# Attention inside a bias stage: two steps there instead of three, loads issued later, the first ten steps in another order

## The chip, the core and the metric

The program runs on one core of a Trainium2 chip. The core has engines that each take their own instructions strictly in the order in which the program lists them: TensorE (PE, its weight loads shown as PEld), VectorE (DVE), ScalarE (ACT), GpSimd (POOL), and the sync engine (SP), which here issues nearly all DMAs. [...] The metric is the device time of one execution in microseconds (us); lower is better.

## What is computed

An attention with a learned position bias, and a two-layer block behind it. Cut to what matters:

```python
B, H, S, D = 4, 8, 576, 64
scores = matmul(q, k.T) / sqrt(D)
psi_rel = log1p(abs(i - j));  psi_i = log1p(max(i, 1))
h = maximum((psi_rel / psi_i)[..., None] @ w1 + b1, 0)      # 32 hidden values for each (i, j)
scores = scores + (h @ w2)                                  # one bias for each head and (i, j)
attn = exp(scores - max); attn = attn / (sum(attn) + 1e-9)
x = (attn @ v), heads side by side                          # 2304 tokens x 512
out = (mish-like gate of (x @ w_in)) @ w_out
```

The bias depends on the head, not on the batch, so it is made once and used four times.

## The kernel before

**Bias stage.** The 576 rows are taken in 36 tiles of 16 rows (`idx` 0 to 35 in the loop at L545 to L567, in the order of `ts`). For tile `idx` four hidden tiles `ht` are made (`make_h`, L524 on VectorE or L522 on ScalarE; a small planner with prices, L508 to L516, decides which: 123 fall to VectorE and 21 to ScalarE), TensorE multiplies them with `w2t` into a PSUM tile `bps` (L554), and `evac` takes that out in two pieces, a left one (L535 on ScalarE; for the last two tiles L533 on VectorE) and a right one (L536, ScalarE), into `bt`, which SP writes to DRAM (`bias_d`, L541). There are two `bps` buffers and eight `bt` buffers. `make_h` runs two tiles ahead of TensorE, `evac` one tile behind it. The bias comes back in five loads, one for each chunk c of 128 query rows (chunk 4 has 64 rows), in the order c = 0, 1, 4, 2, 3 (`load_bias`, three DMAs each). Such a load reads what other DMAs wrote, so SP waits until those writes have landed before it issues it, and everything behind it in SP's list waits too.

**Attention.** The 16 pairs of heads (i; four batches times four head pairs) times five chunks c give 80 steps n. A step has these parts, and the text below calls them so: *scores* (L226 on TensorE, into two PSUM tiles `s`, of which there is just one pair), *reductions* (`add_bias`, L243 on VectorE: adds the bias, takes the row extremes, frees the `s` tiles), *exps* (L258 on ScalarE, two for c < 4, one for c = 4), *turn* (`transposes`, L296 on TensorE, two steps later, then two copies from PSUM, L305, or four smaller ones for c = 4), *ends* (L321, the last 64 columns, and a copy L322), and *products* (`pv_duo`, L335 and L339, on TensorE, into a single PSUM tile `o`, copied out by L342). The c = 0 and 1 of a pair form group 0, the others group 1; each group's products need all of its turns. Turned tiles `main` and `tail` have one buffer for each group, turned PSUM tiles `tp` three, and the tile `pt` of a step with c < 4 three. The three first pairs multiply in plain fp32.

**What sets the order.** The order is written out by hand: the loop of the bias stage places steps 0 to 2 at the tiles in `SOFT_AT` (scores at that tile, reductions one tile later, exps two tiles later), loads at the tiles in `BIAS_AT` and at `load_raw(0)`, `load_raw(1)` (q, k and v of a pair); after it, `step(n)` issues the parts of each step. `split` puts one piece of the conversion of the MLP weights (L125 to L132 on VectorE, L142, L143) into each step from step 5 on, and `ahead` the loads for later pairs.

Of the kernel before, what the change touches and what calls it, by code (L numbers as in the profile page):

```python
# [45 lines left out]
def kernel(ctx: ExitStack, tc, qk, v, wb, w2, w_in, w_out, psia, psi4, rinv, eye, out):  # L46
# [46 lines left out]
    todo, w64, w32 = list(order), [], []  # L93
# [115 lines left out]

    NPAIR = B * HP  # L210
    steps = [(i, c) for i in range(NPAIR) for c in ORDER]
    NS = len(steps)
    pt_t, live, o_t, sums = {}, {}, {}, {}

# [3 lines left out]
    def scores(n):  # L218
        i, c = steps[n]
        hi, lo = qk_t[i]  # L220
        terms = [(hi, hi)] if i < PLAIN else [(hi, hi), (hi, lo), (lo, hi)]
        live[n] = [s_ps.tile([P, 2, 512], F32, name="s") for _ in range(2)]
        for j in range(2):
            for t, (q, k) in enumerate(terms):
                for s, rows in zip(live[n], (TOP, LOW)):
                    pe.matmul(s[:, j, :SH], q[rows, c * P:(c + 1) * P], k[rows, KO + j * SH:KO + (j + 1) * SH],  # L226
                              start=(t == 0), stop=(t == len(terms) - 1))

    def add_bias(n):

        i, c = steps[n]
        bt = bias_t[i // B, c]
        m = st.tile([P, 2], F32, name="m")
        if c < 4:
            pt = pp.tile([P, 2 * S], F32, name="pt")
        else:
            pt = p4p.tile([P, 640], F32, name="pt4")
        for u, s in enumerate(live[n]):
            if c < 4:
                rows, k, sl = slice(0, P), u, slice(u * S, (u + 1) * S)  # L240
            else:
                rows, k, sl = (TOP, LOW)[u], 0, slice(0, S)
            dve.tensor_tensor_reduce(  # L243
                out=halves(pt[rows, sl]), in0=s[rows, :, :SH], in1=halves(bt[rows, sl]),
                scale=-0.125, scalar=BIG, op0=ALU.add, op1=ALU.min, accum_out=m[rows, k:k + 1])
        live[n] = (pt, m)
# [13 lines left out]
    def reciprocals(i):  # L260

        hp, b = divmod(i, B)
        r = sums.pop(i)
        rr = r_pad[i % 2]
        dve.tensor_scalar(r, r, 1e-9, None, op0=ALU.add)
        dve.reciprocal(rr[:, 0:9], r)
        rt = xs.tile([P, 32], F32, name="rt", bufs=2)
        dve.transpose(rt, rr)
        for g in range(4):
            sp.dma_start(out=r_d[b][hp][:, 32 * g:32 * g + 32], in_=rt[32 * g:32 * g + 9])  # L270
# [9 lines left out]
    def place(c):  # L280
        return (0, c * P) if c < 2 else (1, 64 + (c - 2) * P)

    def transposes(n, shared=False):
        i, c = steps[n]
        pt, m = live[n]
        main, tail = turned(i, 0 if c < 2 else 1)
        top, low = (t_ps.tile([P, 512], F32, name="tp") for _ in range(2))
        if c < 4:
            cols = [h * 640 + k * P for h in range(2) for k in range(4)]
        else:  # L290
            cols = [k * P for k in range(4)] + [S - P]
        for k, c0 in enumerate(cols):
            for rows, tp in ((TOP, top), (LOW, low)):
                if c == 4 and rows == LOW:
                    c0 = 64 + k * P if k < 4 else 0
                pe.transpose(tp[:, k * 64:k * 64 + 64], pt[rows, c0:c0 + P], ident[rows, rows])  # L296
        inline = c in (2, 3) or (c < 2 and i == 0)
        if inline:
            copy_end = ends(n)
        if c < 4:  # L300
            off = place(c)[1]
            for g, tp in enumerate((top, low)):
                q0 = off + 64 * g
                copy = dve.tensor_copy if shared and g else act.copy
                copy(main[:, :, :, q0:q0 + 64], tp.rearrange("p (h k q) -> p h k q", h=2, k=4))  # L305
            if inline:
                copy_end()
        else:
            for h, tp in enumerate((top, low)):
                act.copy(main[:, h, :, 0:64], tp[:, :256].rearrange("p (k q) -> p k q", k=4))  # L310
                act.copy(tail[(TOP, LOW)[h], 0:64], tp[(LOW, TOP)[h], 256:320])

    def ends(n):

        i, c = steps[n]
        pt, m = live[n]
        grp, off = place(c)
        tail = turned(i, grp)[1]
        end = t_ps.tile([P, 512], F32, name="tp")
        for h in range(2):  # L320
            pe.matmul(end[h * 64:h * 64 + 64, 0:P], pt[:, 512 + 64 * h:576 + 64 * h], ident, start=True, stop=True)  # L321
        return lambda: act.copy(tail[:, off:off + P], end[:, 0:P])  # L322
# [26 lines left out]
    LAG = 2  # L349
# [25 lines left out]
    def ahead(n):  # L375

        i, x = divmod(n, 5)
        if x == 0 and i + 1 < NPAIR:
            load_raw(i + 1)
        c = {(1, 3): 0, (2, 1): 1, (2, 3): 2, (3, 2): 4, (3, 4): 3}.get((i % B, x))  # L380
        if c is not None and i // B + 1 < HP:
            load_bias(i // B + 1, c)
        if n == NS - 11:
            load_x(0, x0.tile([P, HP, TB], F32, name="xraw"))
        if n == NS - 10:
            x_hi[0], x_lo[0] = (xa_t[:, t].bitcast(F32R) for t in range(2))
            load_r(0, x_lo[0].bitcast(F32), 0, HP)
        if NS - 5 <= n < NS - 1:
            d = n - (NS - 5)
            x, hi, lo = (y[0][:, d] for y in (x_raw, x_hi, x_lo))  # L390
            dve.tensor_tensor(hi, x, lo.bitcast(F32), op=ALU.mult)
            pool.tensor_tensor(x, x, lo.bitcast(F32), op=ALU.mult)
            pool.tensor_tensor(lo, x, hi.bitcast(F32), op=ALU.subtract)
# [9 lines left out]
    def convert(on_act, last):  # L403
# [3 lines left out]
        elif conv and next(conv[0]):  # L407
            conv.clear()
            load_weights()
            if w32 and w32[0][0] in order[:EARLY]:  # L410
                split_weights(pool)

    def step(n):
        i, x = divmod(n, 5)

        def begin():
            if n < NS:
                scores(n)
                add_bias(n)

        def turn():
            if 0 <= n - LAG < NS:
                transposes(n - LAG)
            if x == 4 and i:
                ends(n - 3)()

        def end():
            if 0 <= n - 1 < NS and (n - 1) % 5 == 4:
                reciprocals((n - 1) // 5)
            if n < NS:  # L430
                ahead(n)
                split(n)

        def products():
            todo = {4: (i, 0, (0, 1)), 0: (i - 1, 0, (2, 3) if i < NPAIR else (2, 3, 4)), 1: (i - 1, 0, (4,) if i < NPAIR else ()), 2: (i - 1, 1, (0, 1, 2)),
                    3: (i - 1, 1, (3, 4))}.get(x, (-1, 0, ()))
            j, grp, ks = todo
            if 0 <= j < NPAIR and (j, grp) != (0, 0):
                for k in ks:
                    pv_duo(j, grp, k)  # L440

        if n in (3, 4):
            scores(n)
            if n == 3:
                transposes(0, True)
            add_bias(n)
            exps(n, 0)
            if n == 3:
                transposes(1, True)
            exps(n, 1)  # L450
            if n == 3:
                transposes(2)
            else:
                for k in range(5):
                    pv_duo(0, 0, k)
            end()
            return
        begin()
        turn()
        if n < NS:  # L460
            exps(n, 0)
            exps(n, 1)
        end()
        products()
        if x == 1 and n < NS:
            ends(n - 1)()

# [30 lines left out]

    spent = {"v": 0.0, "a": 0.0}
    maker = {}  # L500
    SOFT_AT = (18, 27, 32)
    BIAS_AT = (12, 20, 24, 30, 37)
    for idx, t in enumerate(ts):
        spent["a"] += 1.0 + (1.9 if idx in SOFT_AT else 0.0)
        spent["v"] += (1.7 if idx in SOFT_AT else 0.0)
        n = reach(t)[2]
# [39 lines left out]
    for idx in range(NB + 2):  # L546
        if idx < NB:
            t = ts[idx]
            make_h(idx + 2)
            n = reach(t)[2]  # L550
            ps = bps.tile([P, 1024], F32, name="bps")
            for a in range(0, n, 512):
                for cg in range(4):
                    pe.matmul(ps[cg * 32:cg * 32 + 32, a:min(a + 512, n)], w2t,  # L554
                              h_t[idx, cg][:, a:min(a + 512, n)], start=True, stop=True)
            bps_t[t] = ps
        if 1 <= idx <= NB:
            evac(idx - 1)
        if idx == 1:
            load_raw(0)  # L560
        if idx in BIAS_AT:
            load_bias(0, ORDER[BIAS_AT.index(idx)])
        for lag, do in enumerate((scores, add_bias, exps)):
            if idx - lag in SOFT_AT:
                for u in range(2 if lag == 2 else 1):
                    do(SOFT_AT.index(idx - lag), *((u,) if lag == 2 else ()))
        if idx == 14:  # L567
            load_raw(1)
    load_weights()
    bias_scope.close()  # L570
# [316 lines left out]
```

## Time and profile before

| | us |
|---|---|
| median of 3 runs | 673.56 |
| lowest and highest of them | 670.41, 674.48 |
| the profiled execution | 672.85 |
| its span, first to last instruction | 670.9 |
| granted TensorE clock, mean over the span | 0.992 |

The profiled execution took 672.85 us, of which 670.9 are the span that the views show; 1.95 lie outside it. Times in the views count from the start of the span. The bias stage fills roughly the first 58 us, then come the other steps of the attention, and the MLP last.

### The profile page before, as it was taken

To read this page: it belongs to the slowest core of one execution; us is meant where nothing else is said; L and a number is where in the kernel's file an instruction comes from. 1 tells how busy PE (TensorE), PEld (TensorE's weight loads), DVE (VectorE), ACT (ScalarE), POOL (GpSimd) and SP (SyncE) were. 2 spreads that over 40 slices of the span, in tenths; PEclk is the share of its full clock that TensorE was granted. 3 is DMA by queue.
4 is the path that set the end of the run, shared out by engine and by line. 5 is a ranking of instruction groups with operands and counts; after the bars stand their busy time and mean duration, and the time that the engine had idled before them with its cause. 6 is when DMAs were issued, how large, how long until landed. Compare 5 with 4: busy or idle time off the path is not lost.

```text
span 670.9 us, 13799 instructions
## 1 busy us (share of the span) xinstructions
PE 646.0 (96%) x5300; PEld 498.6 (74%) x5300; DVE 449.6 (67%) x821; ACT 412.2 (61%) x871; POOL 150.2 (22%) x142
## 2 busy tenths in 40 slices
PE   6878999999999999999999999999999999999997
PEld 3214667777777777778888998788888888888886
DVE  7995777877888785631423364344599877888884
ACT  6995899989999899762433333344474444454441
POOL 0000133333222332601111121102233321133330
PEclk9979999999999999999999999999999999999999
DMA  4997586677667859107448886624664544443300
GB/s 138 303 315 234 170 251 208 212 236 237 219 213 231 271 155 265 33 19 218 150 160 241 260 229 189 210 103 135 211 190 125 157 158 142 144 128 114 101 32 32
DMA packets 100913, 119.65 MB, mean 178 GB/s; under 512 B 15600, under 2 KB 77296, under 8 KB 100848
## 3 DMA queue, kind: packets, MB, share of 16 engines
q1 hardware_dynamic: 98544, 110.59, 52.4%
q0 software_dynamic: 1872, 8.09, 4.0%
q8 instruction: 41, 0.67, 0.4%
q14 instruction: 24, 0.20, 0.1%
q10 hardware_dynamic: 432, 0.09, 0.1%
HBM read 79.47 MB, written 39.28 MB: 177 GB/s over the span
## 4 chain that ended last, share of the span: by engine, by line
PE 81%; DMA 7%; DVE 5%; ACT 4%; issue 2%; SPq 1%; POOL 0%; DVEq 0%; ACTq 0%
PE h L623 27%; PE s L226 10%; PE y L739 8%; PE o L335 8%; PE h L739 8%; PE tp L296 5%; PE y L740 4%; PE h L740 4%; PE tp L321 3%; PE bps L554 3%; DVE ht L524 2%; DMA xa<-r_d 2%; PE o L339 2%; DMA x_d<-x 1%; DMA bias_d<-bt 1%
## 5 line engine op out<-in xcount | busy, mean ns | idle before, releaser
L258 ACT ACTIVATE pt<-pt,m 128x576 f32<-128x576 f32 x144 | 112.1, 789 | 3.6 <-DVE m L243 3.6
L243 DVE CUSTOM_DVE_ANT_0 pt<-s,bias 128x576 f32<-128x576 f32 (+1 forms) x112 | 81.6, 755 | 37.2 <-PE s L226 30.9
L635 ACT ACTIVATE g<-h 128x512 f32<-128x512 f32 x72 | 42.8, 597 | 75.9 <-PE h L623 64.2
L305 ACT COPY main<-tp 128x512 f32<-128x512 f32 x126 | 68.0, 596 | 22.1 <-PE tp L296 22.0
L335 PE MATMUL o<-main,vt 128*64 128x320 f32 (+1 forms) x512 | 74.3, 412 | 0.0
L177 POOL TENSOR_TENSOR qklo<-rawqk,qkhi 128x304 fp32r<-128x304 f32 x52 | 44.0, 871 | 123.5 <-DMA rawqk<-in_qk_dram 115.6
L639 POOL TENSOR_TENSOR g<-g 128x256 f32<-128x256 f32 (+1 forms) x40 | 33.7, 844 | 159.9 <-ACT g L635 151.0
L623 PE MATMUL h<-xa,lc 128*128 128x512 f32 (+1 forms) x288 | 55.5, 354 | 0.0
L296 PEld LDWEIGHTS tp<-ident,pt 64*128 64x128 f32 x1184 | 51.3, 138 | 4.2 <-ACT main L305 1.7
L296 PE MATMUL tp<-ident,pt 64*128 64x64 f32 x1184 | 52.7, 222 | 1.4 <-ACT main L305 1.3
L722 DVE TENSOR_TENSOR gslot<-w,gslot 128x1024 fp32r<-128x1024 f32 x30 | 43.3, 1455 | 15.4 <-ACT gslot L721 15.4
L623 PEld LDWEIGHTS h<-xa,lc 128*128 128x128 f32 x288 | 47.6, 189 | 7.5
L554 PE MATMUL bps<-ht,w2t 128*32 128x512 f32 (+17 forms) x352 | 38.7, 559 | 14.5 <-ACT bt L536 6.1
L722 DVE TENSOR_TENSOR gslot<-quarters,gslot 128x1024 fp32r<-128x1024 f32 x28 | 47.0, 1705 | 7.9 <-ACT gslot L721 7.9
L721 ACT CAST gslot<-w 128x1024 fp32r<-128x1024 f32 x30 | 31.5, 1051 | 30.2 <-DVE w L718 18.2
L721 ACT CAST gslot<-quarters 128x1024 fp32r<-128x1024 f32 x28 | 29.4, 1052 | 32.5 <-DVE quarters L718 20.4
L226 PE MATMUL s<-qkhi 64*128 64x288 f32 x260 | 49.2, 343 | 0.1
L226 PEld LDWEIGHTS s<-qkhi 64*128 64x128 f32 x260 | 28.1, 184 | 25.8 <-DVE m L243 11.0
L335 PEld LDWEIGHTS o<-main,vt 128*64 128x64 f32 x512 | 32.7, 136 | 16.0 <-issue 0.7
L524 DVE TENSOR_SCALAR ht<-at,bb 128x576 f32<-128x576 f32 (+17 forms) x123 | 44.1, 440 | 0.0
L226 PE MATMUL s<-qklo,qkhi 64*128 64x288 f32 x260 | 42.0, 296 | 0.0
L226 PE MATMUL s<-qkhi,qklo 64*128 64x288 f32 x260 | 41.2, 292 | 0.4 <-POOL qklo L177 0.4
(150 smaller groups left out, 1479.4 us busy)
## 6 DMA issues: line engine op xcount, KB each, us to landing
g_d<-g SPq DMA_DIRECT2D x32, 512.0 KB
bias_d<-bt SPq DMA_DIRECT2D x36, 295.5 KB
w<-in_w_in_dram SPq DMA_DIRECT2D x16, 512.0 KB
w<-in_w_out_dram SPq DMA_DIRECT2D x16, 512.0 KB
quarters<-g_d SPq DMA_DIRECT2D x16, 512.0 KB
qkhi<-in_qk_dram POOLq DMA_DIRECT2D x13, 608.0 KB, 4.6
rawqk<-in_qk_dram SPq DMA_DIRECT2D x13, 608.0 KB
w<-g_d SPq DMA_DIRECT2D x15, 512.0 KB
```

Of the source, the lines that this page charges most:

```text
L226: pe.matmul(s[:, j, :SH], q[rows, c * P:(c + 1) * P], k[rows, KO + j * SH:KO + (j + 1) * SH], start=(t == 0), stop=(t == len(terms) - 1))
L243: dve.tensor_tensor_reduce(out=halves(pt[rows, sl]), in0=s[rows, :, :SH], in1=halves(bt[rows, sl]), scale=-0.125, scalar=BIG, op0=ALU.add, ...
L258: act.activation(ps, ps, AF.Exp, bias=m[:, u:u + 1], scale=-1.0, accum_out=sums[i][:, k:k + 1])
L296: pe.transpose(tp[:, k * 64:k * 64 + 64], pt[rows, c0:c0 + P], ident[rows, rows])
L305: copy(main[:, :, :, q0:q0 + 64], tp.rearrange("p (h k q) -> p h k q", h=2, k=4))
L335: pe.matmul(o[h * 64:h * 64 + 64, :w], vt[:, h, k, :], main[:, h, k, :], start=(k == 0), stop=False, **kw)
L524: dve.tensor_scalar(ht[:, :n], at[:, :n], bb[:, k:k + 1], 0.0, op0=ALU.add, op1=ALU.max)
L554: pe.matmul(ps[cg * 32:cg * 32 + 32, a:min(a + 512, n)], w2t, h_t[idx, cg][:, a:min(a + 512, n)], start=True, stop=True)
L623: pe.matmul(h[:, u * n:(u + 1) * n], w_at(f, d)[t], x[:, d, :n], start=(k == 0), stop=(k == 11))
L721: act.copy(hi, src)
L722: dve.tensor_tensor(lo, src, hi.bitcast(F32), op=ALU.subtract)
L739: pe.matmul(o, hi[:, f], wc[m][:, f], start=(f == 0 and m in (0, 1, 3)), stop=False, **kw)
```

## The change

Steps 0 and 1 alone stay in the bias stage, at the tiles 26 and 33 (before: steps 0, 1, 2 at 18, 27, 32). The bias loads move from the tiles 12, 20, 24, 30, 37 to 18, 25, 31, 36, 37, `load_raw(0)` from tile 1 to 12, `load_raw(1)` from 14 to 34. The first ten steps run in the order (pair, chunk) = (0,0), (0,1), (0,4), (1,0), (1,1), (0,2), (0,3), (1,4), (1,2), (1,3) instead of all of pair 0 and then all of pair 1, so chunks 2 and 3 of the bias are first needed at steps 5 and 6 (before: 3 and 4). A new function `opening` issues the steps 2 to 9. The first turns of pairs 0 and 1 have one of their two copies on VectorE, ahead of or behind the reductions. `load_raw(2)` moves from step 5 to step 6. The planner's table counts two steps instead of three and gives as many hidden tiles to each engine as before.

```diff
+    FIRST = 10
+    steps[:FIRST] = [(0, 0), (0, 1), (0, 4), (1, 0), (1, 1), (0, 2), (0, 3), (1, 4), (1, 2), (1, 3)]
...
-    def transposes(n, shared=False):
+    def transposes(n, inline=None, shared=False):
...
-        inline = c in (2, 3) or (c < 2 and i == 0)
+        if inline is None:
+            inline = c in (2, 3)
...
-        if x == 0 and i + 1 < NPAIR:
+        if (n == 6 if i < 2 else x == 0) and i + 1 < NPAIR:
...
+    def opening(n):
+        scores(n)
+        if n < 4:
+            transposes(n - 2, True, True)
+        add_bias(n)
+        if n == 4:
+            transposes(2)
+        if n == 5:
+            for k in (3, 4):
+                pv_duo(0, 0, k)
+        if 5 <= n <= 8:
+            transposes(n - 2, n >= 7, True)
+        exps(n, 0)
+        exps(n, 1)
+        if n == 7:
+            reciprocals(0)
+        ahead(n)
+        split(n)
+        if n == 6:
+            for m in (3, 4):
+                ends(m)()
+        for j, grp, k in {4: [(0, 0, k) for k in range(3)],
+                          7: [(1, 0, k) for k in range(2)],
+                          8: [(1, 0, k) for k in range(2, 5)],
+                          9: [(0, 1, k) for k in range(5)]}.get(n, ()):
+            pv_duo(j, grp, k)
...
+        if n < FIRST:
+            opening(n)
+            return
...
+        if n == FIRST:
+            transposes(7)
...
-    SOFT_AT = (18, 27, 32)
-    BIAS_AT = (12, 20, 24, 30, 37)
+    SOFT_AT = (26, 33)
+    BIAS_AT = (18, 25, 31, 36, 37)
...
-        if idx == 1:
+        if idx == 12:
             load_raw(0)
...
-        if idx == 14:
+        if idx == 34:
             load_raw(1)
```

ScalarE inside the bias stage, around the two exps of step 0 (`pt,sums<-pt,m`). Before, they stand between the evacuations (`bt<-bps`) of the tiles 19 and 20:

```order
L535 ACTIVATE bt<-bps,rinv_t 128x575
L536 ACTIVATE bt<-bps,rinv_t 128x16
L258 ACTIVATE pt,sums<-pt,m 128x576 x2
L522 ACTIVATE ht<-at,bb 128x320
L535 ACTIVATE bt<-bps,rinv_t 128x271
L536 ACTIVATE bt<-bps,rinv_t 128x320
```

After, they stand between those of the tiles 27 and 28:

```order
L540 ACTIVATE bt<-bps,rinv_t 128x383
L541 ACTIVATE bt<-bps,rinv_t 128x208
L260 ACTIVATE pt,sums<-pt,m 128x576 x2
L527 ACTIVATE ht<-at,bb 128x448
L540 ACTIVATE bt<-bps,rinv_t 128x399
L541 ACTIVATE bt<-bps,rinv_t 128x192
```

What moved is the place, eight tiles later; in both an exps pair and one hidden tile are ahead of an evacuation.

ScalarE at the end of the bias stage: the right pieces of the last two tiles (128x96 and 128x80), and the copies of step 0's turn (`main<-tp`). Before, the one exp of step 2 stands ahead of both pieces:

```order
L536 ACTIVATE bt<-bps,rinv_t 128x112
L258 ACTIVATE pt_830,sums<-pt_830,m 128x576
L536 ACTIVATE bt<-bps,rinv_t 128x96
L536 ACTIVATE bt<-bps,rinv_t 128x80
L305 COPY main_889<-tp 128x8x64
L322 COPY tail_890<-tp 128x128
```

After, the two exps of step 1 stand between the pieces:

```order
L541 ACTIVATE bt<-bps,rinv_t 128x112
L541 ACTIVATE bt<-bps,rinv_t 128x96
L260 ACTIVATE pt,sums<-pt,m 128x576 x2
L541 ACTIVATE bt<-bps,rinv_t 128x80
L308 COPY main_878<-tp 128x8x64
L325 COPY tail_879<-tp 128x128
```

What moved is that the last piece of the last tile now follows two exps, and step 2 is no more there.

TensorE in the steps 9 to 11, from one step's scores (`s<-qklo`) to the next. Before, the products (`o<-main`) of group 0 of pair 1 are dealt out over the steps:

```order
L226 MATMUL s<-qklo 128x288 x4
L296 MATMUL tp<-ident,pt_1089 128x64 x10
L321 MATMUL tp<-ident,pt 64x128 x2
L335 MATMUL o<-main_1076,vt 64x256 x4
L226 MATMUL s<-qklo 128x288 x4
L296 MATMUL tp<-ident,pt 128x64 x16
L321 MATMUL tp<-ident,pt 64x128 x2
L335 MATMUL o<-main_1076,vt 64x256 x4
L226 MATMUL s<-qklo 128x288 x4
```

After, all products of group 1 of pair 0 stand between the scores of steps 9 and 10, and two turns (of steps 7 and 8) between those of 10 and 11:

```order
L228 MATMUL s<-qklo 128x288 x4
L338 MATMUL o<-main_956,vt 64x320 x8
L342 MATMUL o<-tail_957,vt 64x320 x2
L228 MATMUL s<-qklo 128x288 x4
L298 MATMUL tp<-ident,pt_1077 128x64 x10
L298 MATMUL tp<-ident,pt 128x64 x16
L324 MATMUL tp<-ident,pt 64x128 x2
L228 MATMUL s<-qklo 128x288 x4
L298 MATMUL tp<-ident,pt 128x64 x16
```

From step 12 on the rows are those of before.

## Rows read from the trace of the kernel before

**Rows 1.** The page: busy time by engine.

```profile
PE 646.0 (96%) x5300; PEld 498.6 (74%) x5300; DVE 449.6 (67%) x821; ACT 412.2 (61%) x871; POOL 150.2 (22%) x142
```

**Rows 2.** VectorE's timeline, bias stage: start, us, instruction, count, [idle before].

```profile
5.23 27.26 DVE L524 TENSOR_SCALAR ht<-at,bb 128x576 f32<-128x576 f32 x74
32.41 0.75 DVE L243 CUSTOM_DVE_ANT_0 pt<-s,xa 128x576 f32<-128x576 f32 x1
...
33.76 10.33 DVE L524 TENSOR_SCALAR ht<-at,bb 128x304 f32<-128x304 f32 x32
44.82 0.76 DVE L243 CUSTOM_DVE_ANT_0 pt<-s,xa 128x576 f32<-128x576 f32 x1 [0.73 <-PE s L226]
...
46.18 6.53 DVE L524 TENSOR_SCALAR ht<-at,bb 128x448 f32<-128x448 f32 x17
53.81 0.75 DVE L243 CUSTOM_DVE_ANT_0 pt<-s,bias 64x576 f32<-64x576 f32 x1 [1.10 <-PE s L226]
```

**Rows 3.** Timeline of ScalarE in the bias stage.

```profile
34.39 0.76 ACT L258 ACTIVATE pt<-pt,m 128x576 f32<-128x576 f32 x1
...
57.90 0.33 ACT L536 ACTIVATE bt<-bps,rinv_t 128x80 f32<-128x80 f32 x1 [1.03 <-DMA bias_d<-bt]
```

**Rows 4.** Timeline of TensorE.

```profile
36.54 7.08 PE L554 MATMUL bps<-ht,w2t 128*32 128x304 f32 x48 [2.03 <-DVE ht L524]
...
49.05 3.15 PE L554 MATMUL bps<-ht,w2t 128*32 128x448 f32 x16 [1.37 <-ACT bt L536]
...
62.24 1.19 PE L226 MATMUL s<-qklo 64*128 64x288 f32 x8
```

**Rows 5.** Windows of 2 us: busy (count) by engine, granted clock, DMA share, GB/s.

```profile
36.00:38.00 2.00, 1.46 (x12) 0.55 (x16) 2.00 (x8) 1.31 (x5) 0.00 (x0) 0.50 0.82 310
42.00:44.00 2.00, 2.00 (x20) 0.56 (x14) 2.00 (x6) 1.63 (x5) 0.00 (x0) 0.81 1.01 319
...
52.00:54.00 2.00, 2.00 (x16) 1.16 (x16) 0.90 (x3) 0.91 (x3) 0.00 (x0) 0.75 0.69 197
```

**Rows 6.** Timeline of VectorE behind the bias stage, steps 3 to 12.

```profile
59.09 0.69 DVE L305 COPY main<-tp 128x512 f32<-128x512 f32 x1 [1.22 <-PE tp L296]
59.69 0.75 DVE L243 CUSTOM_DVE_ANT_0 pt<-s,xraw 128x576 f32<-128x576 f32 x1
...
64.26 0.76 DVE L243 CUSTOM_DVE_ANT_0 pt<-s,bias 128x576 f32<-128x576 f32 x1 [2.53 <-DMA bias<-bias_d]
...
66.82 0.76 DVE L243 CUSTOM_DVE_ANT_0 pt<-s,bias 128x576 f32<-128x576 f32 x1 [1.79 <-DMA bias<-bias_d]
...
74.28 0.75 DVE L243 CUSTOM_DVE_ANT_0 pt<-s,bias 64x576 f32<-64x576 f32 x1 [1.55 <-PE s L226]
...
89.14 0.75 DVE L243 CUSTOM_DVE_ANT_0 pt<-s,bias 64x576 f32<-64x576 f32 x1 [0.39 <-PE s L226]
```

**Rows 7.** Chain that ended last, in order of time: start us, us, what, pieces.

```profile
74.74 1.77 PE o L335 x12
76.51 1.17 PE s L226 x8
77.68 0.49 PE tp L296 x16
78.17 0.69 PE o L335 x4
78.86 0.54 PE o L339 x4
...
81.25 0.86 PE o L335 x8
```

**Rows 8.** Timeline of SP's DMA issues.

```profile
28.94 5.45 SPq L541 DMA_DIRECT2D bias_d<-bt  x6
37.16 0.33 SPq L202 DMA_DIRECT2D xa<-bias_d  x1
...
61.45 0.33 SPq L202 DMA_DIRECT2D bias<-bias_d  x1
```

More of the change, by code (lines that the diff above doesn't have):

```diff
@@ L413, in step @@
     def step(n):
+        if n < FIRST:
+            opening(n)
+            return
         i, x = divmod(n, 5)
[L416 to L442, printed above, removed]
+        if n < NS:
             scores(n)
-            if n == 3:
-                transposes(0, True)
@@ L446, in step @@
             add_bias(n)
[L447 to L459, printed above, removed]
+        if n == FIRST:
+            transposes(7)
+        if n - LAG < NS:
+            transposes(n - LAG)
+        if x == 4:
+            ends(n - 3)()
@@ L462, in step @@
             exps(n, 1)
-        end()
-        products()
+        if n - 1 < NS and x == 0:
+            reciprocals(i - 1)
+        if n < NS:
+            ahead(n)
+            split(n)
+        j, grp, ks = {4: (i, 0, (0, 1)), 0: (i - 1, 0, (2, 3) if i < NPAIR else (2, 3, 4)),
+                      1: (i - 1, 0, (4,) if i < NPAIR else ()), 2: (i - 1, 1, (0, 1, 2)), 3: (i - 1, 1, (3, 4))}[x]
+        if j < NPAIR and (j, grp) != (1, 0):
+            for k in ks:
+                pv_duo(j, grp, k)
         if x == 1 and n < NS:
```

## The prediction

> **What bounds the kernel now.** I read the page first: TensorE is busy for 646.0 of 670.9 us [rows 1], so all that an edit can give is in the 25 us in which it is not, and the change touches only the first 90 us. The timeline of VectorE comes next, because the three groups of hidden tiles in it follow each other without idle time up to 44.1 us [rows 2]: up to there VectorE is the bound, and TensorE waits for it (2.03 us for `ht` [rows 4]). After that the waits alternate: VectorE waits for the scores of steps 1 and 2 (0.73 and 1.10 us [rows 2]), because TensorE is slow. [...] The last evacuation ends at 57.90 + 0.33 = 58.23 us [rows 3]. Then come two waits of VectorE for a bias load (2.53 and 1.79 us [rows 6]). From about step 7 the chain that ended last runs over TensorE piece by piece [rows 7]. So a time by which the reductions of step 12 shift (89.14 us before [rows 6]) carries to the end of the program: from step 12 on the order is the same in both. My sum is the start of those reductions after the change.
>
> **A. The bias stage.** Its 123 hidden tiles on VectorE take 27.26 + 10.33 + 6.53 = 44.1 us [rows 2], as many as before. One c < 4 step's reductions take 33.76 - 32.41 = 1.35 us. After the change only step 0's lie ahead of the last hidden tile (step 1's follow it, step 2's are gone). With no wait, the last hidden tile ends at 5.23 + 44.1 + 1.35 = 50.7 us, where it was 46.18 + 6.53 = 52.71.
>
> But TensorE decides here. Step 0's reductions now stand ahead of the last 21 of these tiles, at 0.384 us each (6.53 / 17): they run from 41.2 to 42.6. Two exps of 0.76 us [rows 3] stand on ScalarE ahead of the evacuation of tile 28, as they did ahead of tile 20's, so that a `bps` buffer comes free at 42.6 + 2.3 = 44.9, counting from 33.76 to 36.54 before (2.8 us [rows 2, 4], which holds the exps, one hidden tile and the evacuation). So TensorE idles some 2.8 us there, against 2.03 before in the same place [rows 4], and I expect the same answer from the clock: 0.50 from about 44.9 on. Before, it took 6.2 us of work to rise the first time (36.54 to the window that begins at 42 and has 0.81), and 4.0 the second (49.05 to the middle of the window with 0.75 [rows 4, 5]). At that clock a tile takes 7.08 / 6 = 1.18 to 3.15 / 2 = 1.57 us [rows 4]; the last tiles are the wide ones. Tiles 28 to 33 and the scores of step 1 then end at 51.3 (clock back after 4.0 us) to 52.4 (6.2), instead of 50.7.
>
> From there: step 1's reductions 1.35, two left pieces on VectorE and their hand-over some 1.4 (estimate), and on ScalarE the two exps of step 1 (1.5), which now stand ahead of the last right piece (0.33 [rows 3]). The last evacuation ends at 55.6 to 56.7, **1.6 to 2.6 us earlier** than 58.23. The turn of step 0 and its VectorE copy follow, 1.46 us as before (58.23 to 59.69 [rows 3, 6]): step 2's reductions start at 57.1 to 58.1, middle 57.6.
>
> [...]
>
> **B. The bias waits.** The 2.53 us wait is only partly for the load: scores of step 4 run until 62.24 + 1.19 = 63.4 [rows 4], so about 0.8 of it is the load alone. With the 1.79 that is **2.6 us** that the loads put on the path [rows 6]. Both go: chunk 2 is first needed at step 5 and chunk 3 at step 6, which I put at 67 and 70.5. The last load was issued at 61.45, 3.2 us behind the last evacuation [rows 3, 8]; 2 us earlier now, and landed (as before: before 66.82, some 4 us after the issue [rows 6, 8]) near 64.
>
> **C. Ten steps instead of nine, in another order.** Before, from step 3's reductions (59.69) to step 12's (89.14) are nine steps, 29.45 us, the 2.6 us of waits in them; the steady part, 74.28 to 89.14 [rows 6], is five steps in 14.86, or 2.97 each. After, ten periods lie between step 2's and step 12's reductions. I took each from what stands on the path in the new order, with the reductions 1.35, scores 1.17 and a tenth for hand-over, a turn 0.49, a VectorE copy 0.60 (59.09 to 59.69), products 1.77, 0.69 and 0.54 for a whole group 1, and 0.86 for eight blocks of group 0 [rows 2, 6, 7]:
>
> Step 2 to 3: the scores wait for step 2's reductions (one pair of `s` tiles), then step 1's turn and its copy on VectorE stand ahead of step 3's reductions: 1.35 + 1.27 + 0.49 + 0.60 and hand-over = 3.85. Step 3 to 4: nothing between, 2.6. Step 4 to 5: on TensorE three product blocks (1.3 at the fp32 pace) and a turn lie ahead of the scores, 3.0. Step 5 to 6: step 6's reductions write the `pt` buffer of step 3, whose ends come late, so 0.5 more than steady, 3.5. Step 6 to 7: 2.6. Step 7 to 8: a turn's copy ahead of the reductions, 3.5; step 8 to 9: 3.1. Step 9 to 10: all products of group 1 of pair 0 in a lump, 3.0, and then the scores, 4.35. Step 10 to 11: two turns at once, 3.2; step 11 to 12: the ends of step 10 wait for ScalarE behind the exps, 3.45. The sum is 33.2 us. The last three, and the 3.5s, are estimates between the steady 2.97 and that plus a turn or an exp (0.49 to 0.76).
>
> **Moved loads** I cost at nothing. The q and k of pair 1, issued behind the write of tile 33 near 52.2, land 3.2 us (the last write, above) to 7 us (the load at 37.16 waited for the write of tile 15, second of the six from 28.94 [rows 8]) after the writes ahead of them: 55.3 to 59.3. They are first needed by step 3's scores, 58.4 to 59.5. Cover is thin at one end, which is rival 2. `load_raw(2)` a step later still has four steps, 12 us.
>
> **Sum.** 57.1 to 58.1, plus 33.2, is 90.3 to 91.3 for step 12's reductions, against 89.14: 1.2 to 2.2 us later, 1.7 in the middle. The stage gives 2 us and the loads 2.6, but step 2 is now behind the stage, and the lumps cost 3.5 us beyond ten steady periods. The profiled execution had 672.85; 672.85 + 1.7 = 674.6. The median is 0.7 above that execution: **675 us**.
>
> **Rival 1, faster: the new order overlaps like the steady stretch.** TensorE has nearly the same work in both orders, so my list of periods may count as idle what fills up. Ten periods of 2.97 are 29.7: step 12's reductions at 57.6 + 29.7 = 87.3, 1.8 us earlier, or 671.7 on the median; if also the clock does not fall, 56.2 + 29.7 = 85.9, or 670.3. For it speaks that TensorE is busy through most of the same stretch; against it the single `s`, `o` and `pt` tiles. Chance 0.30.
>
> **Rival 2, slower: q and k of pair 1 land late.** They come behind all the writes of the stage in SP's list, when the DMA share is 0.69 to 1.01 [rows 5]. If they take the 7 us of the write of tile 15 and another one for their larger size, they land near 60.3; it decides from 58.4 on. Then step 3 starts 1 to 2 us later: 676.7, at most 678.5. Chance 0.15. [...]
>
> **Rival 3: the change doesn't do what it says**, and chunk 3 is still awaited at step 6. It would have to land after 70, 6 us later than above: 2.6 us back at most, 677. Chance 0.05.
>
> **How the numbers follow.** My forecast (0 to +3 us) has 0.50. The range takes in rival 1 down to 670.0 and rival 2 up to 678.5: 670.0 to 678.5. A measurement of this kernel can tell about 1%, 6.7 us, from no change. None of the cases reaches that bound; I leave 0.03 for faster and 0.04 for slower, and 0.93 within 1%.
>
> **What would show it.** The last evacuation ends at 55.6 to 56.7; the clock is 0.50 in windows from about 45 to 50 and only there behind the first tiles; no wait of VectorE for a bias load behind the stage; step 12's reductions (VectorE, the first 64x576 of pair 2) at 90 to 91; the longest periods are step 2 to 3 (3.85) and 9 to 10 (4.35). The prediction is wrong if step 12 starts before 88 (the lumps cost nothing), if TensorE waits for `qklo` at step 3, or if the clock does not fall.

## The result, and the profile after

Over 19 runs of each, the changed kernel takes 676.90 us (median; 672.55 to 681.72) and the kernel before 671.53 (667.23 to 674.71). The ratio is 1.0095 with an interval of 1.0074 to 1.0116: **slower by 0.95%**, some 5.4 to 6.4 us. The forecast was 675 us in a range of 670.0 to 678.5 and a loss of 1.7 us. The time lies in the range, but partly by luck, since two errors cancelled in part: the median of 3 runs from which I started was 2 us above that of 19, and the loss was 3 to 4 times as large as I had it.

The page of the changed kernel says little, as before [rows 1]: TensorE is busy as long as it was, in a span of 675.1 us.

```profile
PE 646.7 (96%) x5300; PEld 501.3 (74%) x5300; DVE 452.3 (67%) x825; ACT 410.7 (61%) x867; POOL 150.0 (22%) x142
```

VectorE's timeline has the steps. The rows at 41.34 and 51.62 are the reductions of the steps 0 and 1 in the bias stage, those from 57.27 on the steps 2, 3, 4, 5, and 94.75 is step 12 (compare [rows 2, 6]).

```profile
41.34 0.74 DVE L245 CUSTOM_DVE_ANT_0 pt<-s,xa 128x576 f32<-128x576 f32 x1
...
51.62 0.76 DVE L245 CUSTOM_DVE_ANT_0 pt<-s,xa 128x576 f32<-128x576 f32 x1 [0.98 <-PE s L228]
...
57.27 0.74 DVE L245 CUSTOM_DVE_ANT_0 pt<-s,bias 64x576 f32<-64x576 f32 x1
...
63.83 0.76 DVE L245 CUSTOM_DVE_ANT_0 pt<-s,xa 128x576 f32<-128x576 f32 x1
...
67.03 0.76 DVE L245 CUSTOM_DVE_ANT_0 pt<-s,xa 128x576 f32<-128x576 f32 x1 [1.76 <-PE s L228]
...
71.25 0.76 DVE L245 CUSTOM_DVE_ANT_0 pt<-s,xraw 128x576 f32<-128x576 f32 x1 [2.77 <-PE s L228]
...
94.75 0.75 DVE L245 CUSTOM_DVE_ANT_0 pt<-s,bias 64x576 f32<-64x576 f32 x1 [1.29 <-PE s L228]
```

Step 2's reductions start at 57.27, inside the forecast 57.1 to 58.1. Step 12's start at 94.75, where 90.3 to 91.3 was forecast and 89.14 was the time before. So the stage came out as worked out, and the ten periods behind it took 37.48 us in place of 33.2. Three of them hold the excess: step 2 to 3 took 6.56 (forecast 3.85), 3 to 4 3.20 (2.6), 4 to 5 4.22 (3.0). The other seven took 23.50 against 23.7.

ScalarE's last evacuation of the stage (forecast to end at 55.6 to 56.7; [rows 3]):

```profile
55.51 0.31 ACT L541 ACTIVATE bt<-bps,rinv_t 128x80 f32<-128x80 f32 x1
```

TensorE's timeline has first the wait in the stage, then what stands in the long periods: the scores of step 3 and those of step 4 (compare [rows 4]).

```profile
45.15 4.09 PE L559 MATMUL bps<-ht,w2t 128*32 128x432 f32 x24 [2.23 <-ACT bt L541]
...
59.84 2.38 PE L228 MATMUL s<-qklo 64*128 64x288 f32 x8 [2.89 <-DMA qklo<-in_qk_dram]
...
64.74 2.46 PE L228 MATMUL s<-qklo 64*128 64x288 f32 x7 [1.05 <-DVE m L245]
```

Step 3's scores waited 2.89 us, and what came last was `qklo`, the q and k of pair 1. Then the scores themselves take twice their time: 2.38 and 2.46 us, where 1.19 was the price [rows 4]. The windows (columns as in [rows 5], the clock is the third number from the end) say why:

```profile
44.00:46.00 2.00, 0.85 (x8) 0.26 (x12) 2.00 (x7) 2.00 (x6) 0.00 (x0) 0.77 1.01 355
46.00:48.00 2.00, 2.00 (x16) 0.32 (x12) 2.00 (x7) 1.47 (x4) 0.00 (x0) 0.50 0.93 293
...
56.00:58.00 2.00, 0.94 (x19) 0.63 (x18) 1.33 (x3) 0.75 (x2) 0.18 (x2) 1.00 0.83 245
58.00:60.00 2.00, 0.16 (x2) 0.19 (x3) 0.79 (x4) 0.87 (x2) 0.00 (x0) 0.68 0.93 331
60.00:62.00 2.00, 2.00 (x10) 1.81 (x11) 0.00 (x0) 0.00 (x0) 0.00 (x0) 0.50 1.04 403
...
68.00:70.00 2.00, 2.00 (x16) 1.00 (x15) 0.48 (x2) 1.77 (x5) 0.00 (x0) 0.76 0.17 66
```

The granted clock falls from 1.00 to 0.50 twice: in the stage at the 2.23 us wait, as expected (0.50 in the window from 46), and a second time in the 2.89 us wait; it is low from the window at 58 (0.68) to the one at 68 (0.76). Before, no window from 54 to 98 was below 1.00; the one from 58:

```profile
58.00:60.00 2.00, 1.58 (x27) 1.08 (x26) 0.91 (x2) 0.98 (x3) 0.18 (x2) 1.00 0.92 278
```

The chain that ended last, in order of time, goes through the load:

```profile
52.84 6.87 DMA qklo<-in_qk_dram
```

and SP's timeline shows where that load was issued, behind all writes of the stage but the last two, and the bias load of chunk 3, at 62.11 (before 61.45 [rows 8]):

```profile
50.52 2.26 SPq L546 DMA_DIRECT2D bias_d<-bt  x3
52.84 0.58 SPq L168 DMA_DIRECT2D qklo<-in_qk_dram  x1
...
54.56 1.80 SPq L546 DMA_DIRECT2D bias_d<-bt  x2
...
62.11 0.32 SPq L202 DMA_DIRECT2D bias<-bias_d  x1
```

No wait of VectorE for a bias load is left behind the stage. The two spans differ by 4.2 us where step 12 differs by 5.6. From step 12 to the end the profiled runs of all kernels here took 577.8 to 582.5 us, though this part is nearly the same in each, so that stretch has a scatter of its own; medians over many runs are what the totals below go by.

### The profile page after: what moved, and what is told of

Read it like the earlier page. It is cut to its first block, busy times and chain, and to the rows that moved or that the text cites. A ratio compares the mean times of both kernels' runs of the same rounds, so it can differ in the third digit from the quotient of the medians.

```text
span 675.1 us, 13814 instructions
## 1 busy us (share of the span) xinstructions
PE 646.7 (96%) x5300; PEld 501.3 (74%) x5300; DVE 452.3 (67%) x825; ACT 410.7 (61%) x867; POOL 150.0 (22%) x142
## 4 chain that ended last, share of the span: by engine, by line
PE 87%; ACT 5%; issue 2%; DVE 2%; DMA 2%; SPq 1%; POOL 0%; ACTq 0%; DVEq 0%
PE h L628 29%; PE s L228 11%; PE o L338 9%; PE y L744 8%; PE h L744 8%; PE tp L298 5%; PE y L745 4%; PE h L745 4%; PE tp L324 3%; PE bps L559 3%; PE o L342 2%; ACT bt L541 1%; ACT pt L260 1%; DMA qklo<-in_qk_dram 1%; ACT bt L540 1%
## 5 line engine op out<-in xcount | busy, mean ns | idle before, releaser
L308 ACT COPY main<-tp 128x512 f32<-128x512 f32 x122 | 66.2, 599 | 27.0 <-PE tp L298 26.0
L559 PE MATMUL bps<-ht,w2t 128*32 128x512 f32 (+17 forms) x352 | 36.8, 524 | 14.4 <-ACT bt L541 8.1
```

## The experiments

Names of steps are those of the kernel description. "Lost clock" is 1 less the mean granted clock, times the span, averaged over the runs of a kernel: 6.1 us in the changed kernel, 3.9 to 4.2 in the kernel before. A ratio stands with its 95% interval; it is taken from all runs and can differ from that of the two medians by some 0.002.

My theory after reading the trace was that the late q and k cost a microsecond of waiting, and the clock that falls in that wait the rest. Rivals: the clock falls without the late load as well, since TensorE has too little work there; or the order of the ten steps is what costs.

**The load put back** to where it was before, and nothing else:

```diff
-        if idx == 34:
+        if idx == 14:
             load_raw(1)
```

> The changed kernel, with q, k and v of pair 1 issued at tile 14 as before. Theory L (the late q and k cost about 1 us of waiting, and the clock that falls in that wait costs some 3.4 us more): step 3's scores start at 58.8 to 59.0, the clock stays at 1.00 from 52 on, step 12's reductions start at 90.4, the time is 672.4 us. Rival G (TensorE's wait for step 2's reductions, 56.9 to 58.8, lets the clock fall even without the late load): scores at 58.8, but clock 0.50 until some 68, time 675.9. Rival O (the order of the ten steps costs the time): 676 to 677.

Measured: 676.69 us, ratio to before 1.0093 (1.0061 to 1.0124), lost clock 5.8. My theory fell. TensorE at step 3 and the windows of this run:

```profile
55.20 0.71 PE L298 MATMUL tp<-ident,pt 64*128 64x64 f32 x15 [1.23 <-ACT bt L541]
55.84 0.44 PE L324 MATMUL tp<-ident,pt 128*64 128x128 f32 x4
57.46 2.62 PE L228 MATMUL s<-qklo 64*128 64x288 f32 x7 [1.18 <-issue]
```

```profile
56.00:58.00 2.00, 0.82 (x5) 0.53 (x4) 1.97 (x4) 0.69 (x2) 0.18 (x2) 0.81 0.95 250
58.00:60.00 2.00, 2.00 (x12) 1.52 (x11) 0.16 (x2) 0.87 (x2) 0.00 (x0) 0.50 0.94 303
...
66.00:68.00 2.00, 2.00 (x17) 1.36 (x16) 0.82 (x4) 1.42 (x5) 0.00 (x0) 0.63 0.03 8
```

There is no wait for `qklo`: the scores start 0.85 us after step 2's reductions do (56.61 here), which free the first `s` tile. Yet the clock falls all the same, and stays at 0.50 for some 10 us. In this run it fell in the second of two waits, of 1.23 and 1.18 us, with a turn of 1.1 us between them. The ten periods took 36.55 us, 0.93 less than with the late load: this is what the load itself cost between these two profiled runs. The profiled run is one of the faster ones of its kernel (672.94 us; the seven went from 671.62 to 679.29).

**Work that only keeps TensorE busy**, in the changed kernel with the late load (26 calls), then with the load at tile 14 (5 calls ahead of step 3's scores; then 5 ahead of step 3's and 5 ahead of step 4's):

```diff
+        if n == 3:
+            o = o_ps.tile([P, 512], F32, name="o")
+            for _ in range(26):
+                pe.matmul(o[:, :P], ident, ident, start=True, stop=True)
         scores(n)
```

> The changed kernel with its late load, and 26 matmuls of the identity with itself (128x128) put on TensorE ahead of step 3's scores; nobody reads their result. They only keep TensorE at work during the wait, at full clock some 2.9 us. If the fallen clock is the larger part of the loss: scores of step 3 still start at 59.8, but take 1.24 us instead of 2.38, clock 1.00, step 12's reductions at 91.4, time 673.5 us. If the clock has no part in it and the wait alone matters: 676.9, or 677 to 678 when the matmuls outlast the wait.

> The changed kernel with q, k and v of pair 1 loaded at tile 14, and 5 matmuls of the identity with itself on TensorE ahead of step 3's scores, 1.2 us by the 0.117 us that each of the 52 pieces took in the long fill; nobody reads their result. Theory G: the clock stays at 1.00 or falls later and for less, time 672 to 674 against 676.7 without them. If a fallen clock is not what costs: 676.7 as without them.

> The changed kernel with q, k and v of pair 1 loaded at tile 14, and 5 matmuls of the identity with itself ahead of step 3's scores and 5 ahead of step 4's, in the two waits for reductions; nobody reads their result. Theory G: the clock stays up in most runs behind the stage, lost clock (1 less the mean clock, times the span) 3 to 4 us instead of 5.8, time 673 to 674.5. If the clock is not what costs: 676 to 677.

The first filling on TensorE:

```profile
55.94 6.07 PE L420 MATMUL o<-ident 128*128 128x128 f32 x52
61.94 1.24 PE L228 MATMUL s<-qklo 64*128 64x288 f32 x8
```

and two of its windows, at the wait in the stage (2.23 us here too) and at the filling:

```profile
46.00:48.00 2.00, 1.58 (x16) 0.16 (x8) 2.00 (x7) 2.00 (x5) 0.00 (x0) 1.00 0.94 275
56.00:58.00 2.00, 2.00 (x20) 2.00 (x19) 1.85 (x5) 0.50 (x3) 0.18 (x2) 1.00 0.94 244
```

This run says little about the time: each call made two pieces of 0.117 us, so the filling ran for 6.07 us instead of 2.9, and step 3's scores started at 61.94, not at the expected 59.8. Median 676.57 us (1.0102, 1.0075 to 1.0130), where 673.5 was expected. It does show the clock: lost clock 2.0, with 1.00 through the whole filled wait; it fell only behind the next wait, 1.33 us ahead of step 4's scores, in the windows 66 to 72. The second gave 675.93 us (1.0073, 1.0043 to 1.0103), lost clock 4.3; the third 674.16 (1.0034, 1.0012 to 1.0056), lost clock 2.6. So one filling is not clear of none and missed its expectation (672 to 674); two came out as expected. With one filling the clock still fell in some of the runs (mean clock 0.989 to 1.000), with two it was at least 0.994 in all. The profiled run of the second kernel is the one whose mean clock was 1.000. VectorE's steps 2 and 12, and a window behind the stage:

```profile
56.93 0.74 DVE L245 CUSTOM_DVE_ANT_0 pt<-s,bias 64x576 f32<-64x576 f32 x1
...
90.34 0.75 DVE L245 CUSTOM_DVE_ANT_0 pt<-s,bias 64x576 f32<-64x576 f32 x1 [1.29 <-PE s L228]
```

```profile
60.00:62.00 2.00, 0.70 (x13) 0.42 (x10) 1.60 (x4) 0.86 (x3) 0.00 (x0) 1.00 0.89 252
```

At full clock (1.00 in the windows of this run from 56 to 80) the ten periods take 33.41 us (the third kernel, with 1.00 from 58 to 80: 59.06 to 92.47, 33.41 again). The forecast was 33.2. So the sum over the periods was right for a granted clock of 1.00, and that the clock would hold was the assumption in it that did not. The filling itself put nothing off: step 3's scores started 0.91 us behind step 2's reductions, against 0.85 without it.

**Useful work in the gap:** step 1's turn ahead of step 3's scores, with the load at tile 14, and with the late load.

```diff
 def opening(n):
+        if n == 3:
+            transposes(1, True, True)
         scores(n)
-        if n < 4:
-            transposes(n - 2, True, True)
+        if n == 2:
+            transposes(0, True, True)
```

> The changed kernel with q, k and v of pair 1 loaded at tile 14, and the turn of step 1 on TensorE ahead of step 3's scores instead of behind them, so that useful work fills the wait for step 2's reductions. Theory G: clock 1.00 from 54 to 70, step 2 to 3 about 3.4 us, time 671 to 673. If TensorE's idle time is not the cause: 676 to 677.

> The changed kernel with its late load of pair 1 (tile 34) and one edit: step 1's turn ahead of step 3's scores. That turn keeps TensorE at work to about 60.3, and q and k land at 59.7, so the late load should cost nothing here and the clock should hold: 672.8 as with the load at tile 14. If the late load costs by itself: 674 to 676, with TensorE waiting for qklo.

With the load at tile 14: 672.77 us (1.0041, 1.0018 to 1.0063), lost clock 4.0. With the late load: 676.20 (1.0067, 1.0044 to 1.0090), lost clock 6.6. The second expectation was wrong: the stage ended earlier in this run (step 2's reductions at 56.49, against 59.09), so the turn was over at 57.70, and TensorE waited again. TensorE with the load at tile 14, and VectorE's steps 2, 3 and 12:

```profile
59.06 0.88 PE L298 MATMUL tp<-ident,pt 64*128 64x64 f32 x16 [0.29 <-ACT main L308]
...
60.24 1.70 PE L228 MATMUL s<-qklo 64*128 64x288 f32 x8
```

```profile
59.09 0.74 DVE L245 CUSTOM_DVE_ANT_0 pt<-s,bias 64x576 f32<-64x576 f32 x1
...
61.51 0.76 DVE L245 CUSTOM_DVE_ANT_0 pt<-s,xa 128x576 f32<-128x576 f32 x1
...
90.69 0.75 DVE L245 CUSTOM_DVE_ANT_0 pt<-s,bias 64x576 f32<-64x576 f32 x1 [1.29 <-PE s L228]
```

and with the late load, with the windows around its wait:

```profile
56.45 0.88 PE L298 MATMUL tp<-ident,pt 64*128 64x64 f32 x16 [0.30 <-ACT main L308]
57.26 0.44 PE L324 MATMUL tp<-ident,pt 128*64 128x128 f32 x4
59.95 2.29 PE L228 MATMUL s<-qklo 64*128 64x288 f32 x8 [2.25 <-DMA qklo<-in_qk_dram]
```

```profile
56.00:58.00 2.00, 1.40 (x24) 0.91 (x20) 1.97 (x5) 0.56 (x2) 0.18 (x2) 0.96 1.04 265
58.00:60.00 2.00, 0.05 (x2) 0.08 (x2) 0.73 (x3) 1.51 (x4) 0.00 (x0) 0.50 0.90 335
60.00:62.00 2.00, 2.00 (x8) 1.18 (x8) 0.00 (x0) 0.00 (x0) 0.00 (x0) 0.50 1.04 402
```

The four kernels form a square: late load 676.9, early load 676.7, late load with the turn ahead 676.2, early load with the turn ahead 672.8. By the medians neither edit alone brings more than 0.7 us, both together 4.1. The lost clock goes the same way (6.1, 5.8, 6.6 and 4.0): with either gap left open it is high, with both closed it is as before the change. That is why putting the load back alone showed nothing, and why it would have been wrong to conclude that the load was harmless.

Three things limit this. The single sides of the square are less sure than its diagonal: by the ratios the step from 676.2 to 672.8 is 1.7 us, with intervals that meet, and the seven runs with the early load spread over 7.7 us. The trace with the late load and the turn ahead doesn't show that the wait for q and k caused the fall: the window from 56 already has 0.96, so by an estimate (at 0.50 for the last 0.16 of its 2 us) the clock fell near 57.84, within 0.2 us of the end of the turn at 57.70. And the turn ahead gives more than the clock: with it the ten periods took 31.60 us at full clock (59.09 to 90.69, 1.00 in the windows from 58 to 80), against 33.41 with the filling, since step 2 to 3 took 2.42 in place of 4.16. So of the 4.95 us by which the ten periods of this profiled run are shorter than those with the early load alone, 3.14 are the clock and 1.81 the better overlap.

**The parts alone, on the kernel before.** The late load (`load_raw(1)` at tile 34); the new order with three steps in the stage and every load where it was (its edit is shown against the changed kernel); two steps in the stage with the old order and the old loads.

```diff
-        if idx == 14:
+        if idx == 34:
             load_raw(1)
```

> The kernel before with one edit, q, k and v of pair 1 issued at tile 34 instead of 14. Pair 1 is first needed by step 5 there, near 69 us. Theory L: no wait for them, 671.5 us, within 0.7. If a late load costs in another way (SP's queue, the bias loads behind it): over 673.

```diff
-    SOFT_AT = (26, 33)
-    BIAS_AT = (18, 25, 31, 36, 37)
+    SOFT_AT = (18, 27, 32)
+    BIAS_AT = (12, 20, 24, 30, 37)
...
-        if n < 4:
-            transposes(n - 2, True, True)
+        if n == 3:
+            transposes(0, True, True)
         add_bias(n)
+        if n == 3:
+            transposes(1, True, True)
```

> The new order of ten steps alone: three steps in the bias stage at the tiles of before, every load where it was before; steps 3 to 9 in the new order. Theory L: the order by itself costs next to nothing; step 3's reductions at 59.7 as before and nine periods of together 29.3 us, step 12's at 89.0, time 671.5 us. Rival O (the order costs most of the 5.4 us): 674 to 677.

```diff
-        if n in (3, 4):
+        if n in (2, 3, 4):
             scores(n)
-            if n == 3:
-                transposes(0, True)
+            if n < 4:
+                transposes(n - 2, True)
...
-    SOFT_AT = (18, 27, 32)
+    SOFT_AT = (26, 33)
```

> The kernel before with two steps in the bias stage alone: tiles 26 and 33 instead of 18, 27, 32, step 2 behind the stage with one turn in each of the steps 2, 3 and 4; the order of steps and every load as before. Theory G (with two steps in the stage TensorE runs out of work at its end, and the clock that falls there costs about 4 us): last evacuation near 55.6, clock 0.50 from some 57 to 66, time 674 to 677. If two steps cost nothing by themselves (chunk 3 is then waited for as before, to about 64): 671, clock 1.00 behind the stage.

The late load alone takes 676.50 us (1.0092, 1.0064 to 1.0121), lost clock 6.9: it costs as much as the whole change, against my theory, though nobody waits for q and k there. VectorE waits for a bias load instead, as the alternative in the expectation had it:

```profile
66.47 0.76 DVE L243 CUSTOM_DVE_ANT_0 pt<-s,bias 128x576 f32<-128x576 f32 x1 [5.24 <-DMA bias<-bias_d]
```

```profile
54.97 0.67 SPq L168 DMA_DIRECT2D qklo<-in_qk_dram  x1
...
63.68 0.33 SPq L202 DMA_DIRECT2D bias<-bias_d  x1
```

```profile
60.00:62.00 2.00, 1.05 (x14) 0.79 (x15) 1.23 (x3) 2.00 (x5) 0.00 (x0) 0.56 0.98 375
```

The load of chunk 3 waits in SP's list until the last writes have landed (before, the last one was issued at 58.26 and took 3.14 us, to 61.40); with q, k and v among the DMAs ahead that is 63.68 instead of 61.45 [rows 8], and VectorE waits 5.24 us instead of 2.53 [rows 6]. Step 4's reductions start 2.21 us later than before (66.47 against 64.26), and step 12's 2.25 later (91.39 against 89.14), so the bias load explains all of the delay in this run. The clock fell too, but ahead of that wait (0.56 in the window from 60; the wait begins at 61.2), and cost nothing in the eight periods behind it: 24.92 us against 24.88. This profiled run is one of the fastest of its six (674.37 us); where the slower ones lose the rest of the 5.4 us no trace shows. The new order alone costs nothing: 670.97 us (1.0008, 0.9985 to 1.0032), step 12's reductions at 88.89 where 89.0 was expected. Two steps in the stage alone take 675.04 (1.0055, 1.0028 to 1.0083), lost clock 6.8, and there the clock falls in a wait of 1.80 us ahead of step 3's scores:

```profile
58.00:60.00 2.00, 1.10 (x4) 0.83 (x6) 1.52 (x5) 0.50 (x2) 0.19 (x2) 0.62 0.51 176
...
66.00:68.00 2.00, 2.00 (x17) 1.64 (x16) 1.23 (x3) 0.43 (x1) 0.00 (x0) 0.50 0.26 96
```

So the order is not what costs. Taking a step out of the stage and loading q and k late cost 3.5 and 5.4 us each when done alone; together, with the new order, they cost 5.4. That the two do not add up fits the traces: with two steps in the stage the clock falls behind it, while the late load alone delays a bias load for which the changed kernel, with chunk 3 first used at step 6, does not wait. The new tiles of the bias loads and of `load_raw(0)` were not run alone.

**A faster version.** From the new order with three steps in the stage I took away the waits that its trace shows: first the ends of steps 3 and 4 go with their turns, then the weight conversion starts at step 6, then step 7's turn moves to step 9, behind the products.

```diff
-            transposes(n - 2, n >= 7, True)
+            transposes(n - 2, True, True)
...
-        if n == 6:
-            for m in (3, 4):
-                ends(m)()
...
-        for _ in range((1 if n > 4 else 0)):
+        for _ in range((1 if n > 5 else 0)):
...
-        if n == FIRST:
-            transposes(7)
+        if n == 9:
+            transposes(7)
```

> The new order with three steps in the stage and all loads as before, and in it the ends of steps 3 and 4 issued with their turns instead of together in step 6. Step 6's reductions wait for the pt buffer that step 3's ends read (0.95 us of idle VectorE, step 5 to 6 takes 3.73 us); if that wait is for the ends, the period falls to about 2.9 and the time to 670.2 us, against 671.0. If ScalarE's exps hold it: no change.

> The new order with three steps in the stage and the ends with their turns, and the conversion of the weights from step 6 on instead of 5, since its first piece waited 0.55 us for its load ahead of step 6's reductions. If that wait was on the path: step 12's reductions 0.5 us earlier, at 86.4 when the clock falls only once in the stage, time 669.2. If the clock's falls in the stage decide: within 0.5 us of 669.7.

> The same as the run with the conversion from step 6, and in it step 7's turn issued in step 9 behind the products of group 1 of pair 0 instead of together with step 8's turn in step 10. TensorE waits for ScalarE's copies some 0.7 and 0.9 us in the steps 10 and 11; if the two turns at once cause that, steps 9 to 12 take 9.7 us instead of 10.7 and the time is 668.3. If the lump of products decides (step 9 to 10 gets longer by the turn, 10 to 11 shorter by as much): no change from the run beside it.

The first: 669.71 us (0.9990, 0.9962 to 1.0019), no difference beyond the noise; step 5 to 6 in 3.33 us, down from 3.73 but not to 2.9. The second: 669.39 (0.9971, 0.9948 to 0.9993); step 5 to 6 took 3.29, so the wait for the weight load was not on the path. The third: 668.38 (0.9953, 0.9933 to 0.9973). VectorE's steps 9 to 12 there:

```profile
76.33 0.76 DVE L245 CUSTOM_DVE_ANT_0 pt<-s,bias 128x576 f32<-128x576 f32 x1 [0.35 <-PE s L228]
...
80.67 0.76 DVE L245 CUSTOM_DVE_ANT_0 pt<-s,xa 128x576 f32<-128x576 f32 x1 [0.98 <-PE s L228]
...
82.98 0.75 DVE L245 CUSTOM_DVE_ANT_0 pt<-s,xa 128x576 f32<-128x576 f32 x1
...
86.15 0.75 DVE L245 CUSTOM_DVE_ANT_0 pt<-s,bias 64x576 f32<-64x576 f32 x1 [1.39 <-PE s L228]
```

They took 9.82 us (10.66 without the move; 9.7 expected). The period with the lump grew from 4.02 to 4.34 and the next fell from 3.29 to 2.31. This version is faster than both kernels: 2.8 us below the one before in the same runs (671.15). In the profiled runs 1.67 us of it are the nine periods from step 3 to 12 (27.78 against 29.45); step 3 itself came 1.32 us earlier (58.37 against 59.69), behind a stage whose program is that of before, so this part is scatter and not owed to the edits.

## Why the prediction was off, step by step

**Bounds and the stage (A): right in the profiled run, in part by luck.** Step 0's reductions came at 41.34 (forecast 41.2), TensorE's wait was 2.23 us (2.8), the clock fell there, the last evacuation ended at 55.82 (55.6 to 56.7), step 2's reductions began at 57.27 (57.1 to 58.1). But I took 0.50, which the window from 36 of before has behind the wait of 2.03 us [rows 4, 5], as the clock's answer to this wait too, and it need not be. Two profiled runs whose program up to there is the same, the long filling and the turn ahead with the late load, have the same 2.23 us wait and 1.00 in every window from 34 to 56. No run shows the 56.2 from which rival 1 counts for this case; the step 2 of these two began at 56.34 and 56.49. Over the profiled runs with two steps in the stage, the tiles of the bias loads and the order of the change, it began at 56.34 to 59.09.

**Bias waits (B): right.** Both are gone in the changed kernel.

**Ten steps (C): the order right, the price too low.** "The sum is 33.2 us" holds at full clock, 33.41 in two kernels; at the clock that was granted it was 36.55, and 37.48 with the late load. The failing step is that I asked of the clock only in the stage, although the sum itself contained the reason: I had 3.85 us for a period in which TensorE has two short pieces of work (it was busy for 1.10 of the 4 us from 56 to 60), and did not ask what the clock does with that. Before, the end of the stage has three steps' work and no window below 1.00 from 54 to 98. By the prediction's own signs it was wrong here: TensorE did wait for `qklo` at step 3, and the clock was 0.50 not only behind the first tiles. What the clock does with a wait these traces do not settle: at the end of the stage and behind it 0.50 came with waits of 0.95 to 2.89 us, in five of six profiled runs two of them with 1.1 to 2.6 us between; but a wait of 1.23 us in the kernel before left 1.00, and the 2.23 us wait in the stage was met by 0.50 in one run and by 1.00 in two.

**"Moved loads I cost at nothing": wrong.** q and k landed at 59.70, 6.87 us after their issue, near the 60.3 of rival 2, which I had given 0.15. The load cost 0.93 us between the two profiled runs, where that rival had 1 to 2 (its upper end of 678.5 does not follow from that: 675 and 2 are 677). What rival 2 lacked was the clock. Loading early is worth something in two of three pairs: with the turn ahead, the early load is worth 3.4 us (676.2 to 672.8), and on the kernel before the late one costs 5.4 (671.1 to 676.5), there by the load behind it. In the changed kernel as it is, the early load is worth 0.2 (676.9 to 676.7), which is within the scatter.

**Rival 1 (overlap like the steady stretch): wrong**, its 29.7 us is not reached at full clock either (33.41, and 31.60 with the turn ahead). **Rival 3: wrong**, the change does what it says.

In numbers: with the load early and both gaps filled, the changed kernel has 674.16 us, 3.0 above the kernel before in the same runs; late load and fallen clock are the remaining 2.7 of the 5.4. Of the 3.0 (2.3 by the ratio) I had forecast 1.7. What the rest of it is was not settled (step 2 to 3 took 4.16 in place of 3.85, but the sum of the ten only 0.2 more than forecast); the scatter of the medians is of that size. Nor is the clock all of the loss: the kernel before loses clock too, in its stage, and the difference is 6.1 less 3.9 to 4.2, or about 2 of the 5.4 us.

## What to carry to other kernels

When work is moved out of a stage that overlaps, price not only the wait that appears but the clock behind it: here the ten periods behind two waits of some 1.2 us on TensorE took 36.55 us, with 0.50 for some 10 us of them, in place of the 33.41 at a clock of 1.00. Where two edits can each open a gap in the same place, undoing one of them can show nothing (676.7 and 676.2 against 676.9 here, and 672.8 with both); try the square of both. And a load is not free because its user is late: behind it in the queue stood a load whose user was not, and VectorE's wait for that one grew from 2.53 to 5.24 us.

## What the runs showed of the hardware that was not expected

The clock fell to 0.50 in a pause of 1.18 us: in the run with the early load TensorE was busy from 55.20 to 56.28 between idle stretches of 1.23 and 1.18 us, and the window from 56 already has 0.81 (at 0.50 from near 57.24, by an estimate from that figure). It then stayed at 0.50 for some 10 us, up to the window from 66 with its 0.63, although TensorE was busy for 6.95 of the 8 us from 58 to 66 (the stage before: 4.0 to 6.2 us after work resumed [rows 4, 5]). In the kernel before, a wait of 1.23 us within step 5's scores (up to 67.64) left it at 1.00 in the windows from 66 and 68. What the clock does differs from run to run of the same kernel: the mean clock of nine runs with one filling went from 0.989 to 1.000, and their times from 672.0 to 679.3 us; so one profiled run can't tell what the clock costs a kernel. In the long filling, at a clock of 1.00, a 128x128 matmul of fp32 appears as two pieces of 0.117 us (52 pieces for 26 calls, 6.07 us).
